# Value rows loaded once and joined on chip, in a chunked attention and soft mixture-of-experts kernel

## The chip, the cores and the metric

One NeuronCore of a Trainium2 chip runs the whole program. The metric is the device time of one execution in microseconds (us), lower is better.

## The reference

Two stages. The first is attention in chunks: 4 batches, 8 heads, 768 positions, 64 values a head. Each chunk of 32 queries sees 64 keys: 8 memory keys, 16 to its left, its own 32 and 8 to its right. The second is a soft mixture of 8 experts with 4 slots each, on 3072 tokens of 512 values.

```python
for c in range(nc):                       # nc = 24 chunks of 32
    k_full = concatenate([mem_k, k[:, :, l_start:r_end]])   # 64 keys
    v_full = concatenate([mem_v, v[:, :, l_start:r_end]])
    a = softmax(scale * q_c @ k_full.T)
    out[:, :, c_start:c_end] = a @ v_full
x = out as (3072, 512)
logits = x @ phi                          # (3072, 32)
slot_input = softmax(logits, axis=0).T @ x
for e in range(8):                        # w1: 8 x (512, 1024), w2: 8 x (1024, 512)
    slot_out[e] = relu(slot_input[e] @ w1[e]) @ w2[e]
return softmax(logits, axis=1) @ slot_out
```

All data are 32-bit floats. The expert weights are 32 MiB, more than half of all that is read.

## The kernel before

**Attention.** The work goes in 12 iterations `n`, each with two units `us[0]`, `us[1]` of 128 queries (4 chunks each, all 8 heads in 4 pairs). Per unit: TensorE forms the scores (`s`, 16 matmuls in the program, 32 records in the trace, as every 32-bit matmul of this size leaves two), VectorE takes the maximum and subtracts (`mx`, `p`), ScalarE does the exponential, TensorE transposes the result (`pt_ps`), ScalarE copies it out (`pt`), TensorE multiplies by the values (`a`), VectorE normalizes into `x` (with `z`, the sums of an iteration), TensorE transposes `x` (`xt_ps`), ScalarE copies that out (`xT`). Every second iteration from n = 3 has the logits (`l`) of four units, and every second one from n = 4 the update of the slot inputs: `dt_ps`, its copy `dT`, from n = 6 a third transpose into the same tile, `D_ps`, `D_sb`. VectorE and ScalarE then have some more small steps (`stats`, `lT`, `cz`, `c`).

**The values' layout.** The two heads of a pair share the 128 partitions: even partitions hold keys of one head, odd ones of the other, each with zeros for the other head (dimension `a` of the slab). The keys of two neighbouring chunks overlap, in the sequence memory, even chunk, odd chunk, by 32 of 64. The slab `v_slab` has a place for the even and the odd chunk (dimension `o`), and the host lays the 64 rows of each out in full, so that the shared 32 are loaded twice. One iteration's values come in two DMAs of 512 KB (`load_v`).

**Weights.** Each expert weight half is a piece of 1 MB; there are 32. They wait in slabs: `NW = 12` own ones and 8 that are tiles of the attention which the last iterations set free (two of `kq`, four of `v`, two of `x`). `load_w` loads one piece an iteration, and more at the end; the 21st piece and those behind it take the slabs that the first expert multiplication (`h`) sets free.

**Order.** All instructions of an engine run in the order in which the program is written (`InOrder`). Every load and store is issued by SyncE's queue (SP) in that order as well: per iteration `load_kq(n + 3)` (q, 512 KB, and k, twice 312 KB), then `load_v(n + 2)`, then `load_w`. `kq` and `v` have two buffers each, so each load waits for the readers of two iterations before. The program has eight completion semaphores for these DMAs, taken in turn, and a DMA waits for the one that used its semaphore before: at most eight are under way.

**Behind the attention** come the last logits and slot inputs, the first expert multiplication `h` with `w1`, the second, `so`, with `w2` (two column blocks of 8 experts), and the output `o`, which is copied into free slabs and stored in 12 DMAs of 512 KB.

Of the kernel before, what the change touches and what calls it, by code (L numbers as in the profile page):

```python
# [43 lines left out]
SCALE = 0.125  # L44
NEG = -1.0e30
PIECE = 2048
NW = 12
NIN = 2


# [16 lines left out]
def tile_attn_softmoe(  # L67
# [23 lines left out]
    sel = cp.tile([P, NSLOT], F32, tag="sel", name="sel")  # L91
    gsum = cp.tile([P, 4, NSLOT], F32, tag="gsum", name="gsum")
    phi_sb = cp.tile([P, NKC, NSLOT], F32, tag="phi", name="phi_sb")
    warm = cp.tile([P, P], F32, tag="warm", name="warm")

    k_in = [t[:, 0:2 * KB].rearrange("p (a g n) -> p a g n", a=2, g=NPAIR) for t in kq_slab]
    q_in = [t[:, 2 * KB:].rearrange("p (u g n) -> p u g n", u=UU, g=NPAIR) for t in kq_slab]
    v_in = [t.rearrange("p a o (u c g d) -> p a o u c g d", u=UU, c=2, g=NPAIR) for t in v_slab]

    def load_q(n):  # L100
        sp.dma_start(kq_slab[n % NIN][:, 2 * KB:], qT[n])
# [70 lines left out]
    load_k(0)  # L172
    load_k(1)
    load_v(0)
    sp.dma_start(phi_sb, phi.rearrange("(kc p) s -> p kc s", p=P))
    load_v(1)
    dve.tensor_reduce(out=sel, in_=ident.rearrange("p (g s) -> p s g", s=NSLOT), axis=AX.X, op=ALU.add)
    pool.tensor_copy(out=gsum, in_=sel.rearrange("p (o s) -> p o s", o=1).broadcast_to([P, 4, NSLOT]))

    pexp, rz, xT = {}, {}, {}  # L180

    def scores(u):
        n, uu = divmod(u, UU)
        k, q = k_in[n % NIN], q_in[n % NIN]
        s_ps = ps.tile([P, H, NKEY], F32, tag="S", name=f"s{u}", bufs=2)
        for g in range(NPAIR):
            for j in range(CPU):
                w0 = (2 * uu + j // 2) * STEP + CHUNK * (j % 2)
                win = k[:, :, g, w0:w0 + NKEY]
                pe.matmul(  # L190
                    s_ps[32 * j:32 * j + 32, 2 * g:2 * g + 2, :],
                    lhsT=q[:, uu, g, 32 * j:32 * j + 32], rhs=win, start=True, stop=True,
                )
        return s_ps

    def softmax(u, s_ps):
        n, uu = divmod(u, UU)
        if u % UPB == 0:
            dve.memset(s_ps[0:32, :, 0:LEFT], NEG)
        if u % UPB == UPB - 1:  # L200
            dve.memset(s_ps[96:128, :, NKEY - RIGHT:NKEY], NEG)
        mx = wk.tile([P, H, 1], F32, tag="mx", name=f"mx{u}")
        dve.tensor_reduce(out=mx[:, :, 0], in_=s_ps, axis=AX.X, op=ALU.max)
        if uu == 0:
            pexp[n] = wk.tile([P, UU, NPAIR, NKEY, 2], F32, tag="p", name=f"p{n}")
        dve.tensor_tensor(
            out=pexp[n][:, uu].rearrange("p g n h -> p g h n"),
            in0=s_ps.rearrange("p (g h) n -> p g h n", h=2),
            in1=mx.rearrange("p (g h) o -> p g h o", h=2).broadcast_to([P, NPAIR, 2, NKEY]),
            op=ALU.subtract,  # L210
        )
        act.activation(out=pexp[n][:, uu], in_=pexp[n][:, uu], func=AF.Exp, scale=SCALE)
# [21 lines left out]
    def values(u, pt):  # L234
        n, uu = divmod(u, UU)
        v = v_in[n % NIN]
        a_ps = ps.tile([P, H, D], F32, tag="A", name=f"a{u}", bufs=2)
        for g in range(NPAIR):
            for j in range(CPU):
                pe.matmul(  # L240
                    a_ps[32 * j:32 * j + 32, 2 * g:2 * g + 2, :],
                    lhsT=pt[:, g, 32 * j:32 * j + 32],
                    rhs=v[:, :, j % 2, uu, j // 2, g, :],
                    start=True, stop=True,
                )
        return a_ps
# [6 lines left out]
        )  # L253

    def transpose_x(u, last=False):
        t_ps = ps.tile([P, NKC, P], F32, tag="T" if last else "X", name=f"xt_ps{u}", bufs=2 if last else 1)
        for kc in range(NKC):
            pe.transpose(t_ps[:, kc, :], x_slab[u // 4 % 2][:, u % 4, P * kc:P * kc + P], ident)
        xT[u] = wk.tile([P, NKC, P], F32, tag="xT", name=f"xT{u}", bufs=5)
        if last:  # L260
            act.copy(out=xT[u][:, 0:2], in_=t_ps[:, 0:2])
            dve.tensor_copy(out=xT[u][:, 2:4], in_=t_ps[:, 2:4])
        else:
            act.copy(out=xT[u], in_=t_ps)
# [97 lines left out]
    for n in range(NUNIT):  # L362
        us = (2 * n, 2 * n + 1)
        last = n + 1 == NUNIT
        Gl = (n - 3) // 2 if n >= 3 and n % 2 == 1 else None
        Gd = (n - 4) // 2 if n >= 4 and n % 2 == 0 else None
        pts = [transpose_p(u) for u in us]
        if n >= 1:
            for u in us:
                normalize(u - 2, a_ps[u - 2])  # L370
        normalizer(n)
        if not last:
            s_ps = [scores(u + 2) for u in us]
        if n + 3 < NUNIT:
            load_kq(n + 3)
        if Gd is not None:
            dispatch_t(Gd)
        if Gl is not None:
            l_ps = logits(Gl)
        if n >= 1:  # L380
            transpose_x(us[0] - 2)
        if not last:
            for u, t in zip(us, s_ps):
                softmax(u + 2, t)
        if Gd is not None:
# [24 lines left out]
    transpose_x(NU - 2)  # L410
    keep_warm(1)
    transpose_x(NU - 1, last=True)
    keep_warm(2)
    dispatch_z(NG - 2)
    l_ps = logits(NG - 1)
    D_ps = dispatch(NG - 2, "A", 2)
# [162 lines left out]
def _layouts(inputs):  # L579
    q, k, v = inputs["q"], inputs["k"], inputs["v"]  # L580

    def stream(x, mem):
        half = CHUNK // 2
        parts = [np.zeros((B, H, LEFT, D), x.dtype), x[:, :, :half]]
        for t in range(half, S, 2 * CHUNK):
            parts += [mem, x[:, :, t:t + 2 * CHUNK]]
        parts.append(np.zeros((B, H, RIGHT, D), x.dtype))
        return np.concatenate(parts, axis=2)

    qT = q.reshape(B, NPAIR, 2, UNITS_B, UU, P, D).transpose(0, 3, 6, 2, 4, 1, 5).reshape(NUNIT, P, QW)  # L590
    ks = stream(k, inputs["mem_k"])
    cols = np.array([[t * PAIRS * STEP + c for c in range(KW)] for t in range(UNITS_B)])
    kT = ks[:, :, cols].reshape(B, NPAIR, 2, UNITS_B, KW, D).transpose(0, 3, 2, 5, 1, 4).reshape(NUNIT, 2, D, KB)

    vs = stream(v, inputs["mem_v"])

    rows = np.array([[STEP * i + CHUNK * o + r for o in range(2) for r in range(NKEY)] for i in range(S // (2 * CHUNK))])
    vw = vs[:, :, rows].reshape(B, NPAIR, 2, UNITS_B, UU, 2, 2, NKEY, D).transpose(0, 3, 2, 7, 6, 4, 5, 1, 8)
    vw = vw.reshape(NUNIT, 2, NKEY, 2, VB)
    w2 = inputs["moe_w2"].reshape(E, NFC, P, NBLK, WB).transpose(3, 0, 2, 1, 4).reshape(NBLK, E, P, NFC * WB)  # L600
    return {"qT": qT, "kT": kT, "vw": vw, "phi": inputs["moe_phi"], "w1": inputs["moe_w1"], "w2": w2}


# [16 lines left out]
```

## Time and profile before

| | |
|---|---|
| time, median of 3 runs | 169.74 us (169.26 to 170.81) |
| time of the profiled execution | 170.3 us |
| its span in the trace | 168.5 us |
| TensorE busy | 139.9 us, 83% |
| VectorE busy | 99.5 us, 59% |
| ScalarE busy | 60.4 us, 36% |
| GpSimd busy | 8.5 us, 5% |
| DMA | 66.84 MB, mean 397 GB/s |
| attention, first scores to last `x` | about 7 to 108 us of the span |
| first expert multiplication | from 116.4 us |
| last weight load issued | at 132.5 us, lands 20.1 us later |

Times in the trace count from the first instruction. The page has busy shares per engine, the span in 40 slices of 4.2 us, the DMA queues (one of SyncE's loads and stores, one by which instructions are fetched), the chain of waits that ended last, and groups of like instructions. "issue" in that chain is time in which the engine waited for nothing that the profile shows. SyncE is not an engine that computes: its rows are the issuing of DMAs.

### The profile page before, as it was taken

To read this page: it belongs to the slowest core of one execution; us is meant where nothing else is said; L and a number is where in the kernel's file an instruction comes from. 1 tells how busy PE (TensorE), PEld (TensorE's weight loads), DVE (VectorE), ACT (ScalarE), POOL (GpSimd) and SP (SyncE) were. 2 spreads that over 40 slices of the span, in tenths; PEclk is the share of its full clock that TensorE was granted. 3 is DMA by queue.
4 is the path that set the end of the run, shared out by engine and by line. 5 is a ranking of instruction groups with operands and counts; after the bars stand their busy time and mean duration, and the time that the engine had idled before them with its cause. 6 is when DMAs were issued, how large, how long until landed. Compare 5 with 4: busy or idle time off the path is not lost.

```text
span 168.5 us, 6123 instructions
## 1 busy us (share of the span) xinstructions
PE 139.9 (83%) x2729; PEld 102.1 (61%) x2729; DVE 99.5 (59%) x216; ACT 60.4 (36%) x129; POOL 8.5 (5%) x13
## 2 busy tenths in 40 slices
PE   7369997895979979995995998889999999887800
PEld 6257885784758866884684766647655565553500
DVE  6566997974929994999498949466300101081620
ACT  5023543714532734371535455431122100070520
POOL 8700000000000000000000202000000000000000
PEclk9995999999999999999999999999999999999995
DMA  5999999999999999999999999999999999999896
GB/s 205 360 387 416 404 375 379 424 424 416 413 425 412 422 415 414 419 413 421 414 417 396 321 364 420 426 408 422 418 422 416 424 416 422 416 404 399 350 407 240
DMA packets 12458, 66.84 MB, mean 397 GB/s; under 512 B 2193, under 2 KB 2193, under 8 KB 6801
## 3 DMA queue, kind: packets, MB, share of 16 engines
q1 hardware_dynamic: 12432, 66.46, 97.1%
q8 instruction: 21, 0.34, 0.8%
q14 instruction: 5, 0.03, 0.0%
HBM read 60.16 MB, written 6.29 MB: 394 GB/s over the span
## 4 chain that ended last, share of the span: by engine, by line
PE 55%; DMA 22%; DVE 7%; issue 6%; POOL 3%; ACT 2%; DVEq 0%; ACTq 0%; POOLq 0%
PE s L61 13%; DMA w<-in_w_dram 12%; PE a L61 10%; PE xt_ps L61 6%; DMA kq<-in_kT_dram 6%; PE h L61 5%; PE pt_ps L61 4%; DMA kq<-in_qT_dram 4%; PE o L61 3%; PE D_ps L61 3%; PE l L61 3%; PE so L61 2%; POOL v L61 2%; PE dt_ps L61 2%; DVE v L61 1%
## 5 line engine op out<-in xcount | busy, mean ns | idle before, releaser
L61 PE MATMUL s<-kq 128*32 128x128 f32 x768 | 27.8, 294 | 6.7 <-issue 3.0
L61 PE MATMUL a<-v,pt 128*32 128x128 f32 x768 | 25.0, 274 | 4.9 <-issue 4.9
L61 PEld LDWEIGHTS s<-kq 128*32 128x32 f32 x768 | 23.1, 119 | 8.3 <-issue 4.9
L61 PEld LDWEIGHTS a<-v,pt 128*32 128x32 f32 x768 | 20.6, 110 | 8.0 <-issue 7.7
L61 ACT COPY xT<-xt_ps 128x512 f32<-128x512 f32 (+1 forms) x24 | 13.8, 576 | 28.4 <-PE xt_ps L61 28.4
L61 ACT ACTIVATE p<-p 128x512 f32<-128x512 f32 x24 | 14.7, 630 | 15.9 <-DVE p L61 15.9
L61 DVE TENSOR_TENSOR x<-a,z 128x512 f32<-128x512 f32 x24 | 15.6, 683 | 3.8 <-PE a L61 3.8
L61 DVE TENSOR_REDUCE mx<-s 128x8 f32<-128x512 f32 x24 | 16.3, 678 | 2.7 <-PE s L61 2.4
L61 DVE TENSOR_TENSOR p<-s,mx 128x512 f32<-128x512 f32 x24 | 16.7, 695 | 0.8
L61 PE MATMUL xt_ps<-ident,x 128*128 128x128 f32 x96 | 15.5, 284 | 0.0
L61 ACT COPY pt<-pt_ps 128x512 f32<-128x512 f32 x24 | 13.0, 590 | 5.5 <-PE pt_ps L61 5.5
L61 DVE TENSOR_REDUCE z<-p 128x16 f32<-128x1024 f32 x12 | 14.5, 1212 | 0.7 <-ACT p L61 0.7
L61 PE MATMUL pt_ps<-ident,p 128*128 128x128 f32 x96 | 13.3, 279 | 1.9 <-issue 1.2
L61 PEld LDWEIGHTS pt_ps<-ident,p 128*128 128x128 f32 x96 | 10.6, 141 | 6.0 <-ACT xT L61 3.4
L61 PEld LDWEIGHTS xt_ps<-ident,x 128*128 128x128 f32 x96 | 10.2, 140 | 4.0 <-issue 2.8
L61 PE MATMUL so<-w,hT 128*32 128x256 f32 x192 | 11.4, 381 | 0.5 <-DMA w<-in_w_dram 0.5
L61 PE MATMUL h<-w,siT 128*32 128x256 f32 x192 | 10.8, 380 | 0.1
L61 PE MATMUL o<-sh,cst 32*128 32x256 f32 x96 | 8.0, 404 | 1.6 <-DVE kq L61 0.6
L61 PEld LDWEIGHTS so<-w,hT 128*32 128x32 f32 x192 | 5.8, 110 | 5.5 <-DMA w<-in_w_dram 1.4
L61 DVE COPY hT<-ht_ps 128x32 f32<-128x32 f32 x8 | 1.2, 186 | 13.3 <-PE ht_ps L61 8.6
L61 PEld LDWEIGHTS h<-w,siT 128*32 128x32 f32 x192 | 6.0, 110 | 4.2 <-DVE siT L61 0.3
L61 PEld LDWEIGHTS o<-sh,cst 32*128 32x128 f32 x96 | 5.3, 184 | 4.3 <-DVE kq L61 1.4
(94 smaller groups left out, 133.5 us busy)
## 6 DMA issues: line engine op xcount, KB each, us to landing
w<-in_w_dram SPq DMA_DIRECT2D x24, 1024.0 KB, 11.8
v<-in_vw_dram SPq DMA_DIRECT2D x24, 512.0 KB, 9.3
kq<-in_kT_dram SPq DMA_DIRECT2D x24, 312.0 KB, 9.3
kq<-in_qT_dram SPq DMA_DIRECT2D x12, 512.0 KB, 9.6
v<-in_w_dram SPq DMA_DIRECT2D x4, 1024.0 KB, 9.8
out_dram<-v SPq DMA_DIRECT2D x8, 512.0 KB, 5.1
kq<-in_w_dram SPq DMA_DIRECT2D x2, 1024.0 KB, 10.1
x<-in_w_dram SPq DMA_DIRECT2D x2, 1024.0 KB, 8.5
```

The costliest lines, as they stand in the source:

```text
L61: return self.tc.keep_in_program_order(f(*args, **kwargs))
```

## The change

- The host lays the keys of an even chunk out in another order: key r and key 32 + r side by side. The even partitions' rows that an even and an odd chunk share then stand on fixed places (partitions with `p % 4` of 2 and 3). The scores' windows of `k` are read in the same order, for odd chunks with the two halves swapped, and the places that are masked move with them.
- Only the even chunk's 64 rows a head (`vw`, two DMAs of 256 KB) and the 32 rows that the odd chunk has alone (`vx`, two DMAs of 128 KB, to every fourth partition) are loaded. An iteration's values are 768 KB in four DMAs where they were 1024 KB in two.
- The odd chunk's rows are put together in a new tile `v_odd` (one, not two buffers), half of it per unit: ScalarE copies the even chunk's half, times 1 on the shared partitions and 0 on the others (`shared`, made by two small VectorE steps), and GpSimd adds the `vx` rows. Each is 128 x 1024 values. `join_v(n + 1, 0)` stands behind `values(us[0])` and `join_v(n + 1, 1)` behind `values(us[1])`, and `join_v(0, ...)` ahead of the first softmax.
- `v_odd` takes the place of one weight slab: `NW = 11`.
- `phi` is laid out by the host in rows of 512 bytes.
- The last transpose of `x` uses two tiles, one for ScalarE's copy and one for VectorE's, and two filling matmuls behind it are gone.

```diff
-NW = 12
+NW = 11
+    v_odd = cp.tile([P, 2, VB], F32, tag="vo", name="v_odd")
...
         for par in range(2):
-            sp.dma_start(t[par:P:2, par], vw[n, par])
+            sp.dma_start(t[par:P:2, par, 0], vw[n, par])
+        for par in range(2):
+            sp.dma_start(t[par:P:4, par, 1], vx[n, par])
+
+    def join_v(n, uu):
+        t = v_slab[n % NIN].rearrange("p a o (u n) -> p a o u n", u=UU)
+        half = v_odd.rearrange("p a (u n) -> p a u n", u=UU)[:, :, uu]
+        act.activation(out=half, in_=t[:, :, 0, uu], func=AF.Copy, scale=shared)
+        pool.tensor_tensor(out=half, in0=half, in1=t[:, :, 1, uu], op=ALU.add)
...
-    sp.dma_start(phi_sb, phi.rearrange("(kc p) s -> p kc s", p=P))
+    sp.dma_start(phi_sb, phi)
...
+    dve.tensor_reduce(out=sel4, in_=ident.rearrange("p (m f) -> p f m", f=4), axis=AX.X, op=ALU.add)
+    dve.tensor_tensor(out=shared, in0=sel4[:, 2:3], in1=sel4[:, 3:4], op=ALU.add)
...
-                win = k[:, :, g, w0:w0 + NKEY]
+                win = k[:, :, g, w0:w0 + NKEY].rearrange("p a (t i) -> p a i t", t=2)
+                if j % 2:
+                    win = win[:, :, :, ::-1]
...
-                    rhs=v[:, :, j % 2, uu, j // 2, g, :],
+                    rhs=(vo_in if j % 2 else v)[:, :, uu, j // 2, g, :],
...
+    for uu in range(UU):
+        join_v(0, uu)
     for u in range(UU):
         softmax(u, scores(u))
...
         a_ps[us[0]] = values(us[0], pts[0])
+        if not last:
+            join_v(n + 1, 0)
...
         a_ps[us[1]] = values(us[1], pts[1])
+        if not last:
+            join_v(n + 1, 1)
...
     transpose_x(NU - 1, last=True)
-    keep_warm(2)
```

On ScalarE, at the start of the program and in the first iteration, before (`p`, exponential; `pt`, copy of the transposed exponentials):

```order
L61 COPY kq_65<-warm 128x1248
L61 ACTIVATE p_182<-p_182 128x512 x2
L61 COPY pt_215<-pt_ps_210 128x512
L61 COPY pt_222<-pt_ps_217 128x512
L61 ACTIVATE p_267<-p_267 128x512 x2
L61 COPY pt_316<-pt_ps_311 128x512
```

and of the change:

```order
L61 COPY kq_65<-warm 128x1248
L61 ACTIVATE v_odd<-v_66,shared 128x2x512 x2
L61 ACTIVATE p_194<-p_194 128x512 x2
L61 COPY pt_227<-pt_ps_222 128x512
L61 COPY pt_234<-pt_ps_229 128x512
L61 ACTIVATE p_279<-p_279 128x512 x2
L61 ACTIVATE v_odd<-v_67,shared 128x2x512 x2
L61 COPY pt_334<-pt_ps_329 128x512
```

The first exponentials now stand behind the first two copies of values, and the `pt` copies of the next iteration behind the next two.

On ScalarE, from the end of an iteration with logits (n = 5; `d`, `stats` are its exponentials of logits) into the next (n = 6), before:

```order
L61 ACTIVATE p_904<-p_904 128x512 x2
L61 ACTIVATE d_915,stats<-l_877,stats 128x128
L61 ACTIVATE stats<-stats 128x1
L61 COPY xT_962<-xt_ps_957 128x512
L61 COPY pt_972<-pt_ps_967 128x512
L61 COPY pt_979<-pt_ps_974 128x512
L61 COPY dT_1027<-dt_ps_1024 128x128
```

and of the change:

```order
L61 ACTIVATE p_946<-p_946 128x512 x2
L61 ACTIVATE d_957,stats<-l_919,stats 128x128
L61 ACTIVATE stats<-stats 128x1
L61 ACTIVATE v_odd<-v_66,shared 128x2x512 x2
L61 COPY xT_1003<-xt_ps_0_1004 128x512
L61 COPY pt_1020<-pt_ps_1015 128x512
L61 COPY pt_1027<-pt_ps_1022 128x512
L61 COPY dT_1075<-dt_ps_1072 128x128
```

`xT`, both `pt` and `dT` stand behind the two copies.

On SP, one iteration's loads, before:

```order
L61 DMA kq_64<-in_qT_dram 128x1024
L61 DMA kq_64<-in_kT_dram 64x1248 x2
L61 DMA v_67<-in_vw_dram 64x2048 x2
L61 DMA w_72<-in_w_dram 128x2048
L61 DMA kq_65<-in_qT_dram 128x1024
```

and of the change:

```order
L61 DMA kq_64<-in_qT_dram 128x1024
L61 DMA kq_64<-in_kT_dram 64x1248 x2
L61 DMA v_67<-in_vw_dram 64x1024 x2
L61 DMA v_67<-in_vx_dram 32x1024 x2
L61 DMA w_73<-in_w_dram 128x2048
L61 DMA kq_65<-in_qT_dram 128x1024
```

An iteration has eight DMAs instead of six, and its values are a quarter smaller.

More of the change, by code (lines that the diff above doesn't have):

```diff
@@ L72, in tile_attn_softmoe @@
     vw: bass.AP,
+    vx: bass.AP,
     phi: bass.AP,
@@ L93, in tile_attn_softmoe @@
     phi_sb = cp.tile([P, NKC, NSLOT], F32, tag="phi", name="phi_sb")
+    sel4 = cp.tile([P, 4], F32, tag="sel4", name="sel4")
+    shared = cp.tile([P, 1], F32, tag="shared", name="shared")
     warm = cp.tile([P, P], F32, tag="warm", name="warm")
@@ L97, in tile_attn_softmoe @@
     q_in = [t[:, 2 * KB:].rearrange("p (u g n) -> p u g n", u=UU, g=NPAIR) for t in kq_slab]
-    v_in = [t.rearrange("p a o (u c g d) -> p a o u c g d", u=UU, c=2, g=NPAIR) for t in v_slab]
+    v_in = [t[:, :, 0].rearrange("p a (u c g d) -> p a u c g d", u=UU, c=2, g=NPAIR) for t in v_slab]
+    vo_in = v_odd.rearrange("p a (u c g d) -> p a u c g d", u=UU, c=2, g=NPAIR)
     def load_q(n):
@@ L198, in softmax @@
         if u % UPB == 0:
-            dve.memset(s_ps[0:32, :, 0:LEFT], NEG)
+            dve.memset(s_ps.rearrange("p h (i t) -> p h i t", t=2)[0:32, :, 0:LEFT, 0], NEG)
         if u % UPB == UPB - 1:
-            dve.memset(s_ps[96:128, :, NKEY - RIGHT:NKEY], NEG)
+            dve.memset(s_ps.rearrange("p h (i t) -> p h i t", t=2)[96:128, :, CHUNK - RIGHT:CHUNK, 0], NEG)
         mx = wk.tile([P, H, 1], F32, tag="mx", name=f"mx{u}")
@@ L255, in transpose_x @@
     def transpose_x(u, last=False):
-        t_ps = ps.tile([P, NKC, P], F32, tag="T" if last else "X", name=f"xt_ps{u}", bufs=2 if last else 1)
-        for kc in range(NKC):
-            pe.transpose(t_ps[:, kc, :], x_slab[u // 4 % 2][:, u % 4, P * kc:P * kc + P], ident)
         xT[u] = wk.tile([P, NKC, P], F32, tag="xT", name=f"xT{u}", bufs=5)
[L260 to L264, printed above, removed]
+        half = NKC // 2 if last else NKC
+        for k0 in range(0, NKC, half):
+            t_ps = ps.tile([P, half, P], F32, tag="T" if last else "X", name=f"xt_ps{u}_{k0}", bufs=2 if last else 1)
+            for kc in range(k0, k0 + half):
+                pe.transpose(t_ps[:, kc - k0, :], x_slab[u // 4 % 2][:, u % 4, P * kc:P * kc + P], ident)
+            if k0:
+                dve.tensor_copy(out=xT[u][:, k0:k0 + half], in_=t_ps)
+            else:
+                act.copy(out=xT[u][:, 0:half], in_=t_ps)
     def logits(G):
@@ L595, in _layouts, with rows @@
     vs = stream(v, inputs["mem_v"])
-    rows = np.array([[STEP * i + CHUNK * o + r for o in range(2) for r in range(NKEY)] for i in range(S // (2 * CHUNK))])
-    vw = vs[:, :, rows].reshape(B, NPAIR, 2, UNITS_B, UU, 2, 2, NKEY, D).transpose(0, 3, 2, 7, 6, 4, 5, 1, 8)
-    vw = vw.reshape(NUNIT, 2, NKEY, 2, VB)
+    def rows(order):
+        at = np.array([STEP * i + order for i in range(S // (2 * CHUNK))])
+        w = vs[:, :, at].reshape(B, NPAIR, 2, UNITS_B, UU, 2, len(order), D).transpose(0, 3, 2, 6, 4, 5, 1, 7)
+        return w.reshape(NUNIT, 2, len(order), VB)
+    r = np.arange(CHUNK)
+    vw, vx = rows(np.stack([r, CHUNK + r], axis=1).reshape(-1)), rows(2 * CHUNK + r)
     w2 = inputs["moe_w2"].reshape(E, NFC, P, NBLK, WB).transpose(3, 0, 2, 1, 4).reshape(NBLK, E, P, NFC * WB)
-    return {"qT": qT, "kT": kT, "vw": vw, "phi": inputs["moe_phi"], "w1": inputs["moe_w1"], "w2": w2}
+    phi = inputs["moe_phi"].reshape(NKC, P, NSLOT).transpose(1, 0, 2)
+    return {"qT": qT, "kT": kT, "vw": vw, "vx": vx, "phi": phi, "w1": inputs["moe_w1"], "w2": w2}
 def kernel(**inputs):
```

## The prediction

> **What bounds the kernel now.** I read the page's first three parts, then the stretches, then the chain of waits, and last the queue's rows at the end.
>
> ```profile
> PE 139.9 (83%) x2729; PEld 102.1 (61%) x2729; DVE 99.5 (59%) x216; ACT 60.4 (36%) x129; POOL 8.5 (5%) x13
> PEclk9995999999999999999999999999999999999995
> DMA  5999999999999999999999999999999999999896
> q8 instruction: 21, 0.34, 0.8%
> ```
>
> The DMA engines are busy from end to end, at some 418 GB/s in the stretches below. Read so, each byte saved is time saved: 12 iterations lose 256 KB each, 3.15 MB, at 0.42 MB/us **7.4 us**. That is the bound of the gain, and I don't believe it, for two reasons: the buffers and TensorE.
>
> Eight iterations in stretches, each from one `pt_ps` to the next (the last of the eight, and the sum):
>
> ```profile
> 92.68:100.49 7.81, 7.45 (x158) 5.48 (x156) 5.36 (x12) 4.52 (x10) 0.97 (x1) 1.00 0.91 335
> sum 68.62, PE 59.82 PEld 46.69 DVE 52.56 ACT 31.61 POOL 0.97; mean PE 7.48 PEld 5.84 DVE 6.57 ACT 3.95 POOL 0.12
> ```
>
> An iteration takes 68.62 / 8 = 8.58 us, of which TensorE is busy 7.48. What is the other 1.1? The chain passes over TensorE through all of this part, with these gaps (the first row from TensorE's timeline, the gap in brackets; the rest from the chain):
>
> ```profile
> 27.83 1.14 PE L61 MATMUL s<-kq 128*32 128x128 f32 x33 [0.99 <-issue]
> ...
> 38.48 1.69 issue
> 45.95 1.23 issue
> 58.95 0.65 issue
> 71.77 0.27 issue
> 77.09 1.34 issue
> 90.09 1.76 issue
> ```
>
> Together 7.9 us, with nothing waited for, and in the midst of runs of like matmuls. Stretches from the end of one to the end of the next:
>
> ```profile
> 40.16:47.18 7.02, 5.79 (x126) 4.79 (x127) 5.61 (x11) 3.46 (x7) 0.00 (x0) 1.00 1.01 418
> 59.60:72.03 12.43, 11.81 (x253) 8.76 (x254) 9.61 (x21) 4.84 (x11) 0.00 (x0) 1.00 1.02 417
> ```
>
> They hold 253 and 507 of TensorE's instructions (both counts added): once or twice 256, less a few records that are missing. The instruction queue moved 0.34 MB in 21 packets, 16 KB each, for 2 x 2729 = 5458 instructions, 260 a packet. So the gaps are **waits for TensorE's own instructions**, which come over the DMA engines that the loads fill. The only lighter stretch, 92.68 to 100.49 (share 0.91, 335 GB/s), has none and takes 7.81 us, 0.36 above its busy time. The Trainium skill ("Runtime: NRT & Kernel Launch", Instruction fetch mechanics) has the blocks of 256 too, but says that the fetch is hidden by the issue floor; the rows above disagree for a full queue.
>
> **The change, part by part.**
>
> *Buffers.* The end of the program hangs on the weights:
>
> ```profile
> 107.51 0.33 SPq L61 DMA_DIRECT2D v<-in_w_dram  x1
> DMA to landing us min/median/max: 7.5/7.5/7.5
> ...
> 117.49 15.39 SPq L61 DMA_DIRECT2D w<-in_w_dram  x12
> DMA to landing us min/median/max: 20.1/20.1/20.1
> ```
>
> The first two rows are the load into `v_slab`'s third place, free once the last values are multiplied; the last row is that of the last weight load, issued at 132.5. A piece takes 1.05 MB / 0.42 = 2.5 us of the queue. At 107.5 the 17th piece is issued and lands 7.5 later, so two are ahead of it and 14 of 32 have landed; the other 18 take 45 us, to 152.5 (the row says 132.5 + 20.1 = 152.6). Now the queue has less to carry, but with `NW = 11` only 15 slabs are free before the last values are. All 15 can have landed at 107.5, then the queue stands idle and starts again. Its start costs, by the program's first load,
>
> ```profile
> L61 SPq DMA_DIRECT2D kq<-in_qT_dram x1: 389/389/389, 0.7 to 0.7; - x1
> DMA to landing us min/median/max: 3.4/3.4/3.4
> ```
>
> 3.4 - 0.52 / 0.42 = 2.1 us. Last weight: 107.5 + 2.1 + 17 x 2.5 = 152.1, **-0.5**, if the attention ends when it did (bounds -2.5 for one piece without the restart, and 0). The stores behind it are the same 6.3 MB. So the 7.4 us are nearly lost to the slabs; whatever moves the attention's end moves the whole end with it.
>
> *Instruction waits.* An iteration's loads are 512 + 624 + 1024 + 1024 = 3184 KB now, 7.8 us of the queue at 418 GB/s, and 2928 KB after, 7.2; and at most eight DMAs are under way, which is one iteration's worth after and a third more before. The queue will have holes, as in 92.68 to 100.49. The gain lies between 0 and 7.9; I take three quarters, nearer to the light row: **-5.9**. One wait of TensorE for a load,
>
> ```profile
> PE s L61 <- DMA kq<-in_kT_dram: 0.7, 1, 0.7
> ```
>
> goes as well, since three value loads ahead of it are 0.26 MB smaller, 1.9 us: **-0.7**.
>
> *Joins.* Prices from the nearest groups and rows:
>
> ```profile
> L61 ACT ACTIVATE p<-p 128x512 f32<-128x512 f32 x24 | 14.7, 630 | 15.9 <-DVE p L61 15.9
> L61 ACT COPY kq<-warm 128x1248 f32<-128x1248 f32 x1 | 1.2, 1232 | 0.0
> L61 POOL MEMSET hT<- 128x1024 f32 x2 | 2.0, 976 | 95.7 <-DVE z L61 95.7
> ```
>
> ScalarE: 0.82 ns an element between the first two, so 1.05 us for 1024. GpSimd has no sum of two tensors here: above one write (0.98), below three passes (2.9), I take 2.2, as it reads two and writes one. The Trainium skill ("GPSIMD Engine Reference", Elementwise) gives 4497 ns for 2048 elements, an estimate of 2.25 for half.
>
> *Start.*
>
> ```profile
> L61 SPq DMA_DIRECT2D v<-in_vw_dram x4: 541/594/601, 4.8 to 7.5; - x4
> DMA to landing us min/median/max: 6.5/8.8/9.4
> ...
> 12.32 0.63 ACT L61 ACTIVATE p<-p 128x512 f32<-128x512 f32 x1 [0.70 <-DVE p L61]
> ...
> 13.77 3.38 PE L61 MATMUL s<-kq 128*32 128x128 f32 x64
> ...
> 18.68 0.63 ACT L61 ACTIVATE p<-p 128x512 f32<-128x512 f32 x1 [0.81 <-DVE p L61]
> ...
> 22.42 1.96 PE L61 MATMUL a<-v,pt 128*32 128x128 f32 x64
> ```
>
> The first value load lands at 4.8 + 6.5 = 11.3; that many bytes are now both `vw` loads. ScalarE waits for it ahead of the exponentials, copies to 13.4, and the second exponential ends at 14.7 instead of 12.95. The scores behind it ran at half clock (PEclk's fourth digit, to 16.8) and end later by less: **+1.1** (bounds 0 and 3: `vx` lands behind). Next, exponentials to 19.3 + 1.1 = 20.4, copies to 21.45 and 22.5, sums to 23.65 and 25.85, and the second unit's values can't end ahead of 26.8, where 22.42 + 1.96 = 24.4 stood: another **+1.3**.
>
> *Later.* ScalarE is idle half the time, but its order matters:
>
> ```profile
> 57.51 0.37 ACT L61 ACTIVATE d<-l,stats 128x128 f32<-128x128 f32 x1
> 57.86 0.28 ACT L61 ACTIVATE stats<-stats 128x1 f32<-128x1 f32 x1
> 58.52 1.08 ACT L61 COPY pt<-pt_ps 128x512 f32<-128x512 f32 x2
> 61.72 0.27 ACT L61 COPY dT<-dt_ps 128x128 f32<-128x128 f32 x1 [2.12 <-PE dt_ps L61]
> ...
> 62.80 1.88 PE a L61 x64
> 63.32 1.18 ACT L61 ACTIVATE p<-p 128x512 f32<-128x512 f32 x2
> ```
>
> With 2.1 us of copies from 58.1, `pt` ends at 61.7 instead of 59.6. The values use it at 62.8 (the chain's row), no loss; `dT` would have come at 61.1 without the gap of 0.65 and comes a microsecond or so later, and TensorE's third transpose into that tile waits for it. Three iterations (6, 8, 10) by 0.8: **+2.4** (0 if the gaps remain, as the wait lies in them). Elsewhere the sums end ahead of the values.
>
> Nothing: `phi`, the two small VectorE steps, the scores' new order (same matmuls; if strided reads cost, 768 x 294 ns is the base). The last transposes' split lies behind the `v_slab` release at 107.5.
>
> **Sum**: -0.5 - 5.9 - 0.7 + 1.1 + 1.3 + 2.4 = -2.3. The span goes from 168.5 to 166.2, the profiled execution from 170.3 to 168.0; from the median of 169.74 the same step gives **167.4**.
>
> **Rivals.**
>
> *The gaps stay* (or come in other places): -0.5 - 0.7 + 1.1 + 1.3 = +1.2, **170.9**. For it: the queue still moves 2928 KB in about 8 us, and a fetch must share an engine with 1 MB loads. The skill's rule that the fetch is hidden would give the same.
>
> *Slower: GpSimd's sums hold VectorE up.*
>
> ```profile
> 60.77 0.18 DVE L61 TENSOR_SCALAR z<-z 128x16 f32<-128x16 f32 x1
> 66.90 0.75 DVE L61 SCALAR_TENSOR_TENSOR D_sb<-D_sb,stats,D_ps 128x512 f32<-128x512 f32 x1 [2.42 <-PE D_ps L61]
> 70.00 0.17 DVE L61 TENSOR_SCALAR z<-z 128x16 f32<-128x16 f32 x1
> ```
>
> Sums at 59.2 to 63.6, and at 65.9 to 70.3 (the exponentials' end at 64.5, 0.3 for `c`, one copy), lie over both `z` steps, which read and write SBUF alone. If such a step waits for the sums, it loses 2.8 and 0.3 in a pair of iterations. The idle 2.42 takes up 1.8 of it once the gap of 0.65 is gone: 1.3 a pair, four pairs, +5.2: **172.6**. With sums of 2.9 it is 4.2 a pair, +17. It decides from where the sums take over 1 us each. Against it: VectorE is busy 6.57 of 8.58. The Trainium skill ("SBUF — State Buffer", Who interferes with whom) has the rule: the two engines share a port pair, and `tensor_scalar` within SBUF and a GpSimd instruction that reads SBUF block each other. No run here shows it.
>
> *All bytes count*: 7.4 less, **162.3**, if the attention ran at TensorE's 7.48 an iteration (8 x 1.1 = 8.8 less).
>
> **Numbers.** Forecast 0.45 (alone 165 to 169.5: gaps by half or all, starts by 1 either way), gaps stay 0.20, slower 0.25, all bytes 0.10. About 1%, 1.7 us, is what a measurement tells from no change. Faster: 0.28 + 0.10 = 0.38; same: 0.17 + 0.13 + 0.01 = 0.31; slower: 0.07 + 0.24 = 0.31. The range, 164 to 174.5, leaves out most of the last case and the long sums.
>
> **What would show it.** The sum of TensorE's "issue" gaps (7.9 to 2); DMA share under 1 between 40 and 107; no weight load under way at the last `v_slab` release; the `v_odd` groups at 1.05 and 2.2 us; `dT` as releaser of `dt_ps`; a `z` TENSOR_SCALAR over 0.18 for the rival. I am wrong if the attention ends outside 103 to 109 on the old scale.

## The result, and the profile after

The changed kernel takes **182.84 us** (median of 4 runs, 181.83 to 184.45) against 170.01 us before: a ratio of **1.076** (95% interval 1.070 to 1.081). Forecast were 167.4 us and a range of 164.0 to 174.5, so sign and range were both missed. In three of the experiments too few runs in the kernel's faster state were left for an interval, so that the median of all runs is given with their spread; the runs to compare with others are 172.17 us (without sums), 182.64 us (the copy from the upper half), and 175.41 and 177.25 us (four small loads).

The page's busy times, and its queue in slices (now 4.5 us each):

```profile
PE 148.1 (82%) x2725; PEld 108.0 (60%) x2725; DVE 116.4 (64%) x218; ACT 84.6 (47%) x153; POOL 64.7 (36%) x37
DMA  6999899999999999998999996099999999999796
GB/s 222 370 310 306 311 333 344 401 416 410 386 409 386 388 361 385 320 368 332 330 329 370 278 362 273 16 340 351 389 403 427 425 418 423 421 385 404 300 408 251
```

VectorE is busy 17 us more, though it has no new work beyond two small steps, and slice 26 moves 16 GB/s: the queue stood empty at the end of the attention. The groups name VectorE's 17 us (behind the first bar the busy us of all and the mean ns of one, behind the second the idle time before them and what ended it):

```profile
L61 POOL TENSOR_TENSOR v_odd<-v_odd,v 128x1024 f32<-128x1024 f32 x24 | 56.3, 2368 | 47.2 <-ACT v_odd L61 47.2
L61 PE MATMUL s<-kq 128*32 128x128 f32 x768 | 31.9, 321 | 3.1 <-DVE shared L61 2.9 <-issue 0.2
L61 ACT ACTIVATE v_odd<-v,shared 128x1024 f32<-128x1024 f32 x24 | 26.1, 1136 | 7.9 <-DMA v<-in_vw_dram 7.9
L61 DVE TENSOR_SCALAR z<-z 128x16 f32<-128x16 f32 x12 | 19.2, 1598 | 0.4
L61 DVE RECIPROCAL z<-z 128x16 f32<-128x16 f32 x12 | 3.0, 253 | 0.4
```

Two of them before:

```profile
L61 PE MATMUL s<-kq 128*32 128x128 f32 x768 | 27.8, 294 | 6.7 <-issue 3.0 <-POOL gsum L61 2.9 <-DMA kq<-in_kT_dram 0.7
L61 DVE TENSOR_SCALAR z<-z 128x16 f32<-128x16 f32 x12 | 2.1, 175 | 0.4
```

The addition of 1e-9 to `z`, 16 numbers a partition, takes 1598 ns where it took 175; RECIPROCAL on the same tile, right behind it, takes 253 as before. Two iterations in the timelines of GpSimd and VectorE, a typical one and the last:

```profile
45.08 4.69 POOL L61 TENSOR_TENSOR v_odd<-v_odd,v 128x1024 f32<-128x1024 f32 x2 [2.72 <-ACT v_odd L61]
46.01 1.46 DVE L61 TENSOR_SCALAR z<-z 128x16 f32<-128x16 f32 x1
...
106.04 4.71 POOL L61 TENSOR_TENSOR v_odd<-v_odd,v 128x1024 f32<-128x1024 f32 x2 [2.93 <-ACT v_odd L61]
109.00 3.56 DVE L61 TENSOR_SCALAR z<-z 128x16 f32<-128x16 f32 x1
110.69 1.84 POOL L61 MEMSET hT<- 128x1024 f32 x2
```

In the first pair the addition ends at 47.47, just as the first of two sums does (45.08 + 4.69 / 2 = 47.43), and slips in ahead of the second. In the last it starts in the second sum and gets no gap until both MEMSETs queued behind are done: 109.00 + 3.56 = 112.56, and 110.69 + 1.84 = 112.53. This wait of VectorE for GpSimd is called the hold below.

Where the 12.8 us of the span went, by stretches. Iterations 3 to 10, from one `pt_ps` to the next (two neighbours and the sum), then the last iteration up to the release of the last value slab, after and before (each row has the stretch, its length, the busy us of TensorE, of its weight loads, of VectorE, ScalarE and GpSimd, then TensorE's granted clock, the DMA share and GB/s):

```profile
60.17:70.45 10.28, 8.95 (x157) 6.06 (x156) 8.56 (x20) 8.41 (x17) 4.78 (x3) 1.00 0.98 379
70.45:77.66 7.21, 7.21 (x181) 6.41 (x178) 6.81 (x11) 3.55 (x6) 4.63 (x2) 1.00 0.95 344
...
sum 69.35, PE 63.54 PEld 49.48 DVE 61.29 ACT 48.23 POOL 37.59; mean PE 7.94 PEld 6.18 DVE 7.66 ACT 6.03 POOL 4.70
...
105.75:117.04 11.29, 7.30 (x119) 5.31 (x116) 8.82 (x15) 4.83 (x12) 6.49 (x4) 0.91 0.56 206
```

```profile
100.49:107.51 7.02, 6.01 (x119) 4.54 (x116) 5.44 (x14) 3.21 (x9) 0.98 (x1) 1.00 1.01 425
```

The eight iterations cost 69.35 us for 68.62: hardly more. VectorE's 61.29 for 52.56 shows the hold, but iterations 5, 7 and 9 are bound by TensorE (7.21 of 7.21 in the second row). The other 12 us lie ahead and behind: iteration 3 begins at 36.40 instead of 31.87 (+4.5), the last iteration takes 11.29 instead of 7.02 (+4.3), and then the weights, in SyncE's queue:

```profile
117.04 0.80 SPq L61 DMA_DIRECT2D v<-in_w_dram  x2
...
L61 SPq DMA_DIRECT2D kq<-in_w_dram x1: 327/327/327, 144.2 to 144.2; - x1
DMA to landing us min/median/max: 21.3/21.3/21.3
```

From the release at 117.04 the last weight takes until 144.2 + 21.3 = 165.5, 48.5 us where it took 45.2 (107.5 to 152.7): +3.3. Sum 4.5 + 0.7 + 4.3 + 3.3 = 12.8.

### The profile page after: what moved, and what is told of

The parts are those of the page before. It is cut to its first block, busy times and chain, and to the rows that moved or that the text cites. A ratio compares the mean times of both kernels' runs of the same rounds, so it can differ in the third digit from the quotient of the medians.

```text
span 181.3 us, 6248 instructions
## 1 busy us (share of the span) xinstructions
PE 148.1 (82%) x2725; PEld 108.0 (60%) x2725; DVE 116.4 (64%) x218; ACT 84.6 (47%) x153; POOL 64.7 (36%) x37
## 4 chain that ended last, share of the span: by engine, by line
PE 37%; DVE 23%; POOL 13%; DMA 12%; ACT 6%; issue 5%; DVEq 0%; ACTq 0%
POOL v_odd L61 13%; DMA w<-in_w_dram 12%; PE a L61 8%; DVE z L61 8%; PE s L61 7%; PE h L61 5%; DVE x L61 3%; PE xt_ps L61 3%; PE o L61 3%; DVE v L61 3%; ACT v_odd L61 3%; PE D_ps L61 3%; DVE p L61 2%; PE so L61 2%; DVE mx L61 2%
## 5 line engine op out<-in xcount | busy, mean ns | idle before, releaser
L61 POOL TENSOR_TENSOR v_odd<-v_odd,v 128x1024 f32<-128x1024 f32 x24 | 56.3, 2368 | 47.2 <-ACT v_odd L61 47.2
L61 PE MATMUL s<-kq 128*32 128x128 f32 x768 | 31.9, 321 | 3.1 <-DVE shared L61 2.9
L61 PEld LDWEIGHTS s<-kq 128*32 128x32 f32 x768 | 26.7, 120 | 6.2 <-POOL gsum L61 3.0
L61 ACT ACTIVATE v_odd<-v,shared 128x1024 f32<-128x1024 f32 x24 | 26.1, 1136 | 7.9 <-DMA v<-in_vw_dram 7.9
L61 PE MATMUL a<-v,pt 128*32 128x128 f32 x384 | 27.3, 282 | 0.9 <-issue 0.9
L61 PE MATMUL a<-v_odd,pt 128*32 128x128 f32 x384 | 26.3, 282 | 2.1 <-POOL v_odd L61 1.9
L61 PEld LDWEIGHTS a<-v_odd,pt 128*32 128x32 f32 x384 | 20.5, 113 | 3.7 <-POOL v_odd L61 3.7
L61 DVE TENSOR_SCALAR z<-z 128x16 f32<-128x16 f32 x12 | 19.2, 1598 | 0.4
L61 PE MATMUL pt_ps<-ident,p 128*128 128x128 f32 x96 | 14.4, 291 | 5.2 <-issue 3.1
L61 DVE COPY v<-o 128x512 f32<-128x512 f32 x8 | 5.2, 686 | 12.2 <-PE o L61 12.2
(101 smaller groups left out, 164.0 us busy)
## 6 DMA issues: line engine op xcount, KB each, us to landing
kq<-in_w_dram SPq DMA_DIRECT2D x4, 1024.0 KB, 21.3
```

The lines of the kernel that those rows point to most:

```text
L61: return self.tc.keep_in_program_order(f(*args, **kwargs))
```

## The experiments

**Theory:** GpSimd's sums hold VectorE's addition to `z`, as the slower rival had it, and the slab that `v_odd` took costs the rest. **Rivals:** ScalarE's copies, the strided windows of `k`, too few bytes in the queue. Names beginning with `a_` are the kernel after with an edit, with `b_` the kernel before.

### The hold taken away

`a_nozadd`:

```diff
-        dve.tensor_scalar_add(zf, zf, 1e-9)
```

> The kernel after without the addition of 1e-9 to the sums z of the exponentials (each is at least 1, so that the addition changes nothing in fp32). Theory 1 (GpSimd's sums hold that addition up, 1598 ns for 175 before, in each of 12 iterations): the waits go, RECIPROCAL stays at 253 ns, the iterations are 1.0 to 1.4 us shorter, the last value slab is released near 105 to 108 instead of 117, and the time is 171 to 174 us. Rival 1 (the hold passes to the next VectorE instruction within SBUF): RECIPROCAL takes 1.6 us, the time stays at 181 to 184. Rival 2 (the wait lay beside TensorE's work, what costs is the strided scores and ScalarE's copies): RECIPROCAL at 253 ns and the time within 2 us of 182.8.

174.98 us (1.024 of before, 1.016 to 1.033). **Some 8 of the 12.8 us are gone** (182.84 - 174.98 = 7.9) with an instruction that adds nothing, and RECIPROCAL, now the one that follows the same reduction, is not held in its place:

```profile
L61 DVE RECIPROCAL z<-z 128x16 f32<-128x16 f32 x12 | 3.0, 253 | 0.4
...
101.72:109.90 8.18, 6.18 (x119) 4.69 (x116) 6.89 (x14) 4.04 (x11) 6.00 (x4) 0.93 0.80 310
```

The last iteration alone is 3.1 us shorter (8.18 for 11.29). It is not free of the hold, which has passed on to two later steps. In the chain of this run:

```profile
105.40 0.55 DVE stats L61
...
106.38 1.37 DVE cz L61
```

Before, these two took 0.16 and 0.17 us. The first, a TENSOR_TENSOR, ends with GpSimd's sums (101.22 + 4.72 = 105.94), the second, a TENSOR_SCALAR, with the MEMSETs behind them (105.87 + 1.85 = 107.72).

`b_nozadd`: the same line out of the kernel before.

> The kernel before without the addition to z, output whole: the control for the run of the kernel after without it. Theory (the addition by itself costs 175 ns in a chain that is not the bound): within 0.7 us of 169.7. Rival (it stands on the path in 12 iterations): 167.6.

169.75 us (0.999, 0.996 to 1.003): without sums the addition costs nothing.

`a_nosum`:

```diff
-        pool.tensor_tensor(out=half, in0=half, in1=t[:, :, 1, uu], op=ALU.add)
```

> The kernel after without GpSimd's sums; the odd chunks then lack half of their value rows in the output. Theory 1: the addition to z is back at 175 to 180 ns and the time is that of the variant without the addition, or up to 2 us below it: 169 to 174. Rival (copies on ScalarE and the strided scores cost the 12.8 us): z is short again and the time stays over 178.

175.33 us (172.17 to 177.26). The spread covers that of `a_nozadd`, and the addition is back at 174 ns: what the sums cost is, within this spread, the hold.

### The hold put into the kernel before

`b_copies` and `b_join`, with `NW = 11`, at the places of `join_v` (`scratch` is read by nobody; the second has the last line as well):

```diff
+        half = scratch.rearrange("p a (u n) -> p a u n", u=UU)[:, :, uu]
+        act.activation(out=half, in_=t[:, :, 0, uu], func=AF.Copy, scale=SCALE)
+        pool.tensor_tensor(out=half, in0=half, in1=t[:, :, 1, uu], op=ALU.add)
```

> The kernel before with 11 slabs, and ScalarE's two copies of 128x1024 in each iteration at the places of the kernel after, onto a scratch tile that nothing reads (with a constant scale); loads, windows and values as before, no sums, output whole. Base is the run with 11 slabs, 172.5. Theory (the copies delay the first exponentials, pt and dT in ScalarE's queue, 2.6 us as between the runs without sums and without joins): 174.5 to 176. Rival (copies cost nothing beside a full queue of loads): 172 to 173.

> As the run with the copies alone, and GpSimd's sums behind them on the same scratch tile; nothing else of the change is in it, output whole. Theory (sums alone hold VectorE's addition to z): z at 1.3 to 1.7 us and 6 to 9 us more than with the copies alone, 181 to 184. Rival (the hold needs the kernel after's loads or windows): z at 175 ns and the time of the copies alone.

176.93 us (1.041, 1.033 to 1.050) and 183.67 us (1.078, 1.070 to 1.085). Groups of the first, then of the second:

```profile
L61 DVE TENSOR_SCALAR z<-z 128x16 f32<-128x16 f32 x12 | 2.1, 175 | 0.4
```

```profile
L61 DVE TENSOR_SCALAR z<-z 128x16 f32<-128x16 f32 x12 | 14.3, 1189 | 0.4
```

Sums alone, on a kernel with all its loads, contiguous windows and no `v_odd`, make the hold: +6.7 us, and as nobody reads their result, no wait for it is in this. The copies' price was more than expected, 4.4 over the run with 11 slabs, and all of it is the start: the first two copies wait for whole 512 KB loads, and the first `pt_ps` stands at 15.28 instead of 10.98 with 11 slabs alone. Iterations 3 to 10 take 69.27 us, and 69.82 with 11 slabs alone: in the middle the copies cost nothing.

### What is held, and for how long

`a_ztt`:

```diff
-        dve.tensor_scalar_add(zf, zf, 1e-9)
+        dve.tensor_tensor(out=zf, in0=zf, in1=eps, op=ALU.add)
```

> The kernel after with the addition to z kept, but as TENSOR_TENSOR with a tile of 1e-9 instead of TENSOR_SCALAR with a constant: same operands within SBUF, same place, same size. Theory 1 (what GpSimd's sums hold is the TENSOR_SCALAR form; RECIPROCAL and TENSOR_TENSOR on SBUF kept their times in the kernel after): some 160 to 200 ns each, time 174 to 176. Rival (any VectorE instruction at that place, the first behind the sums' start, is held): 1.4 to 1.7 us each and 181 to 184.

My theory 1 fell: 179.15 us (1.056, 1.052 to 1.060), and

```profile
L61 DVE TENSOR_TENSOR z<-z,eps 128x16 f32<-128x16 f32 x12 | 16.8, 1400 | 0.4
L61 DVE RECIPROCAL z<-z 128x16 f32<-128x16 f32 x12 | 3.0, 253 | 0.4
```

The sum of two SBUF operands is held as well, RECIPROCAL with one is not, nor `z`'s own reduction (1.21 us in both kernels). The rival's "any instruction" is too wide too (`a_nozadd`). The Trainium skill ("SBUF — State Buffer", Who interferes with whom) says that a VectorE instruction with two SBUF inputs contends with a GpSimd instruction that reads SBUF, not with one that only writes it; that `tensor_scalar` can enter two-port modes, which contend with GpSimd; and that an instruction with at most one SBUF input outside these modes does not contend. The rows agree, the last iteration too, where the two forms differ. GpSimd's MEMSETs have no input. Here TENSOR_TENSOR starts at 109.25 and takes 1.54 us, to the end of the sums (106.03 + 4.72 = 110.75), though the MEMSETs run on to 112.53; TENSOR_SCALAR in the kernel after waited for these as well, to 112.56. The last `x` step then starts at 114.64 us instead of 117.04, most of the 3.7 us by which this run is shorter. That TENSOR_SCALAR ran in a two-port mode is inferred; no row names the mode.

`a_sum4`:

```diff
+        for i in range(4):
+            at = slice(128 * i, 128 * i + 128)
-        pool.tensor_tensor(out=half, in0=half, in1=t[:, :, 1, uu], op=ALU.add)
+            pool.tensor_tensor(out=half[:, :, at], in0=half[:, :, at], in1=t[:, :, 1, uu, at], op=ALU.add)
```

> The kernel after with each sum of 128x1024 cut into four of 128x256, addition to z kept, output whole. Theory (VectorE gets in when the running GpSimd instruction ends): z waits 0.3 us on the mean instead of 1.4, at most 0.65, and the time is 175.5 to 178. Rival (VectorE must wait until GpSimd has nothing queued): z at 2 us or more and 183 or above.

179.44 us (1.045, 1.033 to 1.057).

```profile
L61 POOL TENSOR_TENSOR v_odd<-v_odd,v 128x256 f32<-128x256 f32 x96 | 66.7, 733 | 36.7 <-ACT v_odd L61 35.4 <-PE xt_ps L61 1.3
L61 DVE TENSOR_SCALAR z<-z 128x16 f32<-128x16 f32 x12 | 5.2, 433 | 0.4
```

The wait shrinks with the length of one GpSimd instruction: 433 - 175 = 0.26 us with 733 ns, 1.42 us with 2368 ns. The median is above the expected 175.5 to 178, but the interval, 175.3 to 179.4 us, doesn't tell it apart. Four short sums take 2.93 us instead of 2.37; what that costs was not tried.

### The slab, the windows, the copies, the bytes

`b_nw11`:

```diff
-NW = 12
+NW = 11
```

> The kernel before with 11 weight slabs instead of 12. At the last release of a value slab 14 pieces had landed and two were queued; with 15 usable slabs one is still queued, so the queue does not run dry and the last weight lands as before: within 0.5 us of 170.0. Rival (each slab is worth a piece, 2.5 us): 172.5.

172.50 us (1.015, 1.009 to 1.020): the rival. The ten microseconds from the release, in this run and before:

```profile
107.70:117.70 10.00, 9.41 (x110) 6.36 (x114) 5.91 (x21) 2.63 (x9) 0.00 (x0) 1.00 0.92 360
```

```profile
107.50:117.50 10.00, 9.41 (x110) 6.36 (x114) 5.92 (x21) 2.63 (x9) 0.00 (x0) 1.00 0.99 415
```

One piece less queued ahead, and the queue has holes where it had none.

`a_flat`, then `a_zflat`, which lacks the addition to `z` as well:

```diff
-                win = k[:, :, g, w0:w0 + NKEY].rearrange("p a (t i) -> p a i t", t=2)
-                if j % 2:
-                    win = win[:, :, :, ::-1]
+                win = k[:, :, g, w0:w0 + NKEY]
```

> The kernel after with the scores' k windows read in natural order, without stride and without reversal; the keys then stand in another order than the values, so the output differs. Theory (strided windows make a pair of 32 score matmuls 2.42 us instead of 1.95): the pairs are back at 1.95 us. If they stand on the path between two iterations, 11 x 0.45 = 5 us go, to 178; if VectorE's hold is the later one of the two, less than 1 us goes. Rival (the matmuls are slower for another reason, clock or queue): the pairs stay at 2.4 us and the time at 182.8.

> The kernel after without the addition to z and with the scores' k windows in natural order (keys then in another order than the values, so the output differs). Theory 1 (with the hold gone TensorE is the bound of an iteration, and 64 strided score matmuls cost it 64 x 30 ns = 1.9 us in two pairs of units): up to 11 x 0.9 us go from 175.0, at least 3: 168 to 172. Rival (VectorE's chain or the queue sets the iteration): 173.5 to 175.

181.97 us (1.071, 1.063 to 1.079) and 173.36 us (1.019, 1.014 to 1.024): 0.9 and 1.6 us less than their bases, which the spread of the runs covers. `b_stride` puts the three lines into the kernel before.

> The kernel before with the k windows read at stride 2, and in reverse for odd chunks, nothing else (the keys then stand in another order than the values, so the output differs). Theory (the stride alone makes a score matmul 318 ns for 288): the score group is at 315 to 320 ns and the time 1 to 5 us over 170.0. Rival (the 318 ns come of something else in the kernel after): 286 to 290 ns and 170.0.

170.61 us (1.006, 1.003 to 1.010), 0.8 us. Score groups of `a_flat` and `b_stride`:

```profile
L61 PE MATMUL s<-kq 128*32 128x128 f32 x768 | 25.4, 288 | 2.8 <-POOL gsum L61 2.8
```

```profile
L61 PE MATMUL s<-kq 128*32 128x128 f32 x768 | 32.5, 319 | 4.6 <-POOL gsum L61 2.9 <-issue 1.7
```

The strided order (key r, then 32 + r, so that neighbours stand 32 values apart) does cost TensorE 25 to 33 ns a record. The records overlap, so the price is in the busy time, 32.5 us for 27.8 before, some 5 us. It costs little of the time: in `b_stride` TensorE waits less for its instructions, as the next rows show. Waits of `a` and `s`, before, and in `b_stride`:

```profile
PE a L61 <- issue: 4.9, 4, 1.8
PE s L61 <- issue: 3.0, 3, 1.3
```

```profile
PE a L61 <- issue: 3.3, 3, 1.5
PE s L61 <- issue: 1.7, 4, 0.7
```

`a_nojoin` (copies and sums out) and `a_fix` (`a_nozadd`, and these lines moved):

```diff
     for u in range(UU):
         softmax(u, scores(u))
+    for uu in range(UU):
+        join_v(0, uu)
```

> The kernel after without ScalarE's copies and without GpSimd's sums (v_odd is set to zero once; the odd chunks' share of the output is left out). Loads, slabs and strided windows stay. Theory (copies cost at the start alone, some 2 us): 172 to 174, against 175.3 with the copies. Rival 1 (the copies cost in each iteration too): 168 to 171. Rival 2 (copies cost nothing): 175.

> The kernel after without the addition to z, and with the first unit's two joins behind its exponentials instead of ahead of them; the output is whole. Theory (ScalarE's copies ahead of the first exponentials cost the start 1.8 to 2.3 us, which carries through): 172 to 173.5, first pt_ps at 11.7 instead of 13.5. Rival (the join comes later by as much as the exponentials come earlier, and the values of the second iteration wait): 174.5 to 176.

`a_nojoin` takes 172.39 us (1.013, 1.006 to 1.019): **with the join free of charge the change is still slower**, by about 1%. The joins without their hold cost 175.0 - 172.4 = 2.6 us, with what was passed on of it. `a_fix` takes 174.35 us (1.027, 1.022 to 1.031), not told apart from `a_nozadd`: the first `pt_ps` is at 11.54, but the second iteration's at 19.78 instead of 19.88; the copies are late either way.

`b_bytes`, the smaller loads alone:

```diff
-            sp.dma_start(t[par:P:2, par], vw[n, par])
+            sp.dma_start(t[par:P:2, par, 0], vw[n, par])
+        for par in range(2):
+            sp.dma_start(t[par:P:4, par, 1], vx[n, par])
```

> The kernel before with only the first 32 rows of the odd chunks' tile loaded (every second row of a head's partitions, so that they lie over all 128 partitions); nothing is joined, the odd chunks' other rows stay zero and their share of the output is left out. 12 slabs, natural windows: the smaller loads alone. Theory (the queue is no longer full, TensorE's waits for its instructions go, the attention ends near 101 to 103 instead of 107.5, and the queue then runs dry and restarts): 164 to 167. Rival 1 (the bytes bring nothing, since slabs hold the end): 169 to 170. Rival 2 (all bytes count): 162.5.

169.36 us (0.998, 0.992 to 1.003): **3.15 MB less bring nothing**. Its waits:

```profile
PE a L61 <- issue: 4.1, 3, 1.9
PE s L61 <- issue: 3.3, 5, 1.2
```

7.4 us where there were 7.9: this lighter queue (378 GB/s between 40 and 95 us for 409) does not feed TensorE its instructions sooner.

### A join without sums

A join without GpSimd has no hold and needs no `v_odd`. (`half` starts from the kernel after, with the windows in two runs of 32 keys.) In `half` the shared rows stand in partitions 64 to 127, `vx` lands in partitions 0 to 63 of the odd chunk's own tile, ScalarE copies the rest; no `v_odd`, 12 slabs.

```diff
-            sp.dma_start(t[par:P:4, par, 1], vx[n, par])
+            sp.dma_start(t[par:P // 2:2, par, 1], vx[n, par])
...
+        act.copy(out=t[P // 2:P, :, 1, uu], in_=t[P // 2:P, :, 0, uu])
...
-    vw, vx = rows(np.stack([r, CHUNK + r], axis=1).reshape(-1)), rows(2 * CHUNK + r)
+    vw, vx = rows(np.concatenate([r, CHUNK + r])), rows(2 * CHUNK + r)
```

> A repaired join, whole output: the shared 32 rows of a chunk pair lie in partitions 64 to 127 of the even chunks' tile, the 32 further rows are loaded straight into partitions 0 to 63 of the odd chunks' tile (the slab's second half, as before), and ScalarE alone copies the shared 64 partitions over; no sum on GpSimd, no v_odd, 12 weight slabs, the k windows in runs of 32 keys, and in the first iteration the copies stand behind the exponentials. Theory (the time went to the hold of VectorE, 7.9 us, to the slab, 2.6, to strided scores and the start): z is back at 175 ns, score pairs at 1.95 us, the last value slab is released by 104 to 108, the time is 166 to 171. Rival 1 (ScalarE's copies of 2 x 1.1 us an iteration hold up the exponentials or pt): 172 or more. Rival 2 (fewer bytes bring all of the 7.4 us): 163 to 165.

186.07 us (182.64 to 188.0), no better than the change itself. Three kernels of loads alone tell why; they are `b_bytes` with the rows of `vx` at other places.

```diff
# b_bytes_low
+            sp.dma_start(t[par:P // 2:2, par, 1], vx[n, par])
# b_bytes_quart
+                sp.dma_start(t[64 * b + par:64 * b + 32:2, par, 1], vx[n, par, 16 * b:16 * b + 16])
# b_bytes_four
+                sp.dma_start(t[64 * b + par:64 * b + 64:4, par, 1], vx[n, par, 16 * b:16 * b + 16])
```

> As the run with half of the odd chunks' rows, but the 32 rows go into partitions 0 to 63 instead of being spread over all 128. Nothing else differs. Theory (a load into the lower half alone takes the 16 DMA engines out of step and slows all loads, as in the repaired join, where an 8 KB packet took 472 ns for 313): some 325 GB/s between 40 and 90, waits of TensorE for instructions, 178 to 186. Rival (the repaired join was slow for ScalarE's copies or its windows of two runs): as the other run, within 1 us.

> As the two runs with the first 32 rows of the odd chunks' tile alone, but the rows go into partitions 0 to 31 (16 rows, one in two of a head's) and 64 to 95 (the other 16), in four DMAs of 64 KB instead of two of 128 KB. Output as there. The Trainium skill (SBUF - State Buffer, Door 1: The DMA port swizzle) has partitions 0 to 63 on 8 of 16 DMA ports, and 0 to 31 with 64 to 95 on all 16. Theory (the lower half is slow because it reaches half of the ports): some 380 GB/s as with the spread rows, 169 to 171. Rival (any block of partitions is slow, as it takes the DMA engines out of step): 320 to 340 GB/s, 180 to 186.

> The control for the run with the rows in partitions 0 to 31 and 64 to 95: the same four DMAs of 64 KB, but to the spread places (every second row of a head's partitions, 16 rows in the lower and 16 in the upper half). Theory (blocks of partitions slow the loads, even over all 16 ports): 375 to 385 GB/s between 40 and 95 us, 8 KB packets at 320 to 330 ns, 169 to 171. Rival (the slowness of that run is that of four small DMAs in place of two, as at most eight are under way): 350 to 360 GB/s, 176 to 178.

185.12 us (1.089, 1.082 to 1.096), 177.10 us (1.039, 1.030 to 1.048) and 178.46 us (175.41 to 181.66). The stretch from 40 to 95 us in `b_bytes`, `b_bytes_low`, `b_bytes_quart` and `b_bytes_four` in turn (the last two numbers are the DMA share and GB/s):

```profile
40.00:95.00 55.00, 49.51 (x1104) 39.17 (x1097) 45.77 (x99) 25.62 (x59) 0.97 (x1) 1.00 0.96 378
```

```profile
40.00:95.00 55.00, 42.80 (x834) 33.52 (x834) 33.83 (x73) 20.00 (x47) 0.00 (x0) 0.88 1.02 321
```

```profile
40.00:95.00 55.00, 46.02 (x1048) 36.41 (x1045) 42.59 (x95) 25.50 (x58) 0.00 (x0) 1.00 0.97 354
```

```profile
40.00:95.00 55.00, 47.65 (x1061) 37.99 (x1052) 41.53 (x88) 24.58 (x55) 0.00 (x0) 0.97 0.93 351
```

In the lower half the engines are busy all the time (1.02) and move 321 GB/s: the transfers themselves are slow, and not those of `vx` alone. Packets of 8 KB, which only the weights have there, take some 0.45 us in this stretch, where they take 0.32 in `b_bytes`. The other two move 354 and 351. `b_bytes_four` has the places of `b_bytes`, and its 175.41 and 177.25 us are not told apart from the 176.11 to 178.39 of `b_bytes_quart`. So what both pay comes of four small DMAs in place of two (ten an iteration, with at most eight under way), and no price of the block of partitions shows. In which way small DMAs cost this is not shown: the engines idle more in `b_bytes_four` (0.93 for 0.96), but not in `b_bytes_quart` (0.97). The Trainium skill ("SBUF — State Buffer", Door 1: The DMA port swizzle) puts partitions 0 to 63 on 8 of 16 ports, and 0 to 31 with 64 to 95 on all; these rows agree. No version came out that beats the kernel before.

## Why the prediction was wrong, by its own steps

The largest step that failed: the sum put GpSimd's hold on VectorE at nothing, on the ground that VectorE has idle time (busy 6.57 of 8.58), and the runs price it at 7.9 of the 12.8 us. Without it the change is still some 5 us slower (`a_nozadd`), where 2.3 us of gain were forecast: the 5.9 from instruction waits did not come, and the slab that was to gain 0.5 cost 2.6. Most of the named signs did not tell: the issue gaps fell to 1.1 us, the DMA share lay at 0.97 from 40 to 95 us and the queue was empty at the release, all as forecast, beside a slower kernel. The two that did are `z` over 0.18 and the attention's end, 117.0 where 103 to 109 was set.

- **The 7.4 us of bytes** were not believed, rightly: `b_bytes` gains 0.2.
- **Buffers, -0.5.** At the release every piece that had a slab had landed and the queue stood empty, as forecast. But a slab less costs 2.6 by itself (`b_nw11`), and from the release the end took 3.3 us more instead of less: I let the queue run full at 2.5 us a piece behind the restart, and it has holes (318 GB/s in the ten microseconds from 117.0). The wait for `kq` (-0.7) is gone, but `b_nozadd` with all its loads has none either, and `a_nozadd` has 3.1 us: no gain of smaller loads is shown.
- **Instruction waits, -5.9, the step that failed first.** I took the waits to come from the load on the queue. With the smaller loads alone they stay (`b_bytes`). In the kernel after they are gone, but TensorE is busy for longer (63.54 us in eight iterations for 59.82) and waits for other things, so nothing is won. The slower scores are not what took them away, as `a_flat` has 288 ns a record and 0.8 us of them. GpSimd's sums with their hold can: 8.2 us in `b_copies`, 2.0 in `b_join`. But `a_zflat`, without hold and stride, has 1.1, so the cause stays open. In the kernel after:

```profile
PE a L61 <- issue: 0.9, 2, 0.5
PE s L61 <- issue: 0.2, 1, 0.2
```

- **Start, +2.4 together**: the first `pt_ps` is 2.3 us later (13.99 for 11.72), and iteration 3 is 4.5 later; without the hold, 2.2 (34.09 for 31.87). The size was right, the hold came on top.
- **Later, +2.4 from `dT`.** Waits for `dT` rose from 1.6 to 2.7 us, but the copies cost nothing in the middle iterations (`b_copies`). That the sums end ahead of the values was wrong: the chain passes over two sums each in iterations 6, 8 and 10 (from 63.11, 80.71 and 98.42, 4.7 us each), and TensorE's values wait for them:

```profile
PE a L61 <- POOL v_odd L61: 1.9, 3, 1.0
```

- **Windows at nothing**: some 30 ns a record that I had dismissed as "same matmuls"; 0.8 us of time in `b_stride`, up to 1.6 in the others. The base was not 768 x 294 ns either, as records overlap, but the group's 27.8 us busy.
- **The prices of a copy (1.05) and of a sum (2.2)** measured 1.14 and 2.37 us.
- **The slower rival** had the mechanism and the instruction right, at a chance of 0.25, but not the size. It let the step wait for both sums; in 11 of 12 iterations it ends with the one that is running. I looked only at the iterations where VectorE has idle time to give, 1.3 us a pair; it is held in every one, and the last iteration, 3.1 us of it, I didn't price. Worse, I kept my gains in its sum: 172.6 less the gains that never came (5.9 and 0.7) would have been 179.2, with the slab at +2.6 for -0.5 182.3, and the measurement is 182.8. That these meet is partly luck: the sum has 5.2 for a hold of 7.9, and +2.4 for `dT`, which no run shows. The range was too narrow because the cases were taken one at a time.

From the runs: bytes, slab and windows together 2.6 us (`a_nojoin`), joins 2.6, hold 7.9: 13.1 for 12.8 measured. They are steps of one row of runs, from before to after, so that they add up proves nothing; what confirms the hold apart from them is `b_join` (6.7 us).

## What to carry to other kernels

Before work is moved to GpSimd, list VectorE's instructions that will overlap it and have two inputs in SBUF, or are a TENSOR_SCALAR within SBUF, the smallest too: what counts is not their length but that of the GpSimd instruction they wait for and how tight VectorE's chain is there. A busy queue doesn't make bytes the bound: test the smaller loads alone, with nothing joined, before building the join. And when a rival changes the cause, rework the whole sum under it, gains included.

## What was not expected of the hardware

- TensorE's waits for instructions were 5.0 us instead of 7.9 with slower score matmuls (`b_stride`), and 7.4 with a lighter queue (`b_bytes`).
- A VectorE TENSOR_SCALAR of 175 ns waits for GpSimd's MEMSETs as well (3.56 us in all), a TENSOR_TENSOR of the same size does not (1.54).
- A matmul record whose moving operand is read alternately from two places 32 values apart takes 318 to 321 ns; in natural order it takes 286 to 299.
- A load to 64 adjacent partitions slows the loads around it: 321 GB/s against 378, for 256 KB in 2.9 MB an iteration.
- Two DMAs of 128 KB cut into four of 64 KB cost some 6 to 8 us (175.41 and 177.25 for 169.36), at the same places in memory.
